# Channel attention and a gated convolution: eleven more rows of squares are summed on GpSimd instead of VectorE

## The chip, the cores and the metric

The kernel runs on one core of a Trainium2 chip. The metric is device time in microseconds (us) from one launch to its end. A time is the median of several runs; the profile and the trace come from one further execution of the same kernel, which has its own time.

## The reference

q, k and v have 4 batches of N = 6336 rows and C = 256 channels, in float32. The attention is over channels, so its matrix is 256x256 for a batch, and it can only be known when all 6336 rows of q and k of that batch have been read.

```
qn = q / (norm(q over rows) + 1e-6)          # one norm for each channel
kn = k / (norm(k over rows) + 1e-6)
s  = kn^T @ qn / tau                         # 256 x 256
a  = exp(s - max(s)); a /= sum(a) + 1e-9     # softmax over a row
x  = v @ a
gate = sigmoid(causal convolution of x over 5 rows, one filter for each channel)
out  = (gate * (x @ w_val)) @ w_out
```

## The kernel before

**Scores.** The rows of q and k of a batch are read as 49 rows for each of 128 partitions, and a rest of 64 rows. They are cut into 17 groups: group 0 has one row of 128 partitions and the rest, groups 1 to 16 have three rows each. `score_group` (lines 167 to 234) handles one group. For the later batches (1 to 3) it splits each row in a high and a low part: ScalarE casts the group to `hi` (L193), GpSimd subtracts for the low part (L194). TensorE multiplies three products for each half of the channels and each row into `s_ps` (L227), which stays in one bank for the whole batch. The norms need the sum of the squares of all rows: ScalarE squares the group into `sq` (L210, for the first row of a sum directly into the sum, L206), and the rows of `sq` are added up (L215) in one of two sums. The first `nv` rows of a group go to VectorE and its sum `acc_ps` in PSUM, the others to GpSimd and its sum `acc` (`side`) in SBUF. Line 175 sets `nv`: 1 in groups 1 to 4 of batch 1, and 2 in all other groups of the later batches.

**Softmax.** `softmax(b)` (L237 to L301) follows the last group of a batch: the two sums are added (L241), a matmul with ones sums them over the partitions (L246, L248), ScalarE takes the root (L253), VectorE the reciprocals (L258, L259), `nk` (L261), the scaled scores `s` (L264) and their minimum `m` (L266). ScalarE takes the exponential of the two halves of `s` (L269), VectorE adds 1e-9 to the sums `z` (L271) and inverts them (`rz`, L273), ScalarE scales to `a` (L276). TensorE transposes `a` in two pairs of matmuls with `ident` (L286), ScalarE copies the result to `at` (L290), and TensorE multiplies it with `w_val` (L295).

**Convolution.** The rows of v go through in 13 chunks of up to 508 rows for each batch, 52 steps in all. A step holds `conv` of the next chunk (L353: products `x_ps`, L346, in two buffers; ScalarE's first tap, L360; four more taps on VectorE, L362), the sigmoid of this chunk on ScalarE (L368), `value` (products `val_ps`, L346; VectorE multiplies the gate, L375), `split_g` (ScalarE casts `g_hi`, L388, GpSimd subtracts for `g_lo`, L389), the transposes of a coming chunk (`t_ps`, L336; `v_hi` on ScalarE, L337, `v_lo` on VectorE, L338), and `finish` of the chunk before (products `o_ps`, L405; ScalarE copies `o_sb`, L415).

**Order.** The main loop (L529 to L564) spreads the groups of the later batches over the first 36 steps, and each call of `tick()` issues one stage of a softmax at a raised priority. The order on each engine is not the order of the code: a scheduler places each instruction by its own model of their times, once, when the kernel is built. A change of one instruction's engine can so move others on all engines. On the chip each engine runs its instructions strictly in that order. Where ScalarE goes from one of Sqrt, Exp and Sigmoid to another, a table load (ACT_TABLE_LOAD, put down to the line of the function) stands ahead of the function.

Of the kernel before, what the change touches and what calls it, by code (L numbers as in the profile page):

```python
# [18 lines left out]
GROUP = 3  # L19
LEAD = 5  # L20
PREFETCH = 4
AHEAD = 2
VLEAD = 2
SIDE = 11
HALO = 4
# [4 lines left out]
def kernel(  # L30
# [25 lines left out]
    a_p = ctx.enter_context(tc.tile_pool(name="a_p", bufs=2))  # L56
    v_p = ctx.enter_context(tc.tile_pool(name="v_p", bufs=VLEAD + 1))
    w_p = ctx.enter_context(tc.tile_pool(name="w_p", bufs=2))
# [108 lines left out]
    def score_group(b, g):  # L167


        n = groups[g][1]  # L170
        raw = raws.pop((b, g))
        if b == 0:
            nw, nv = (GROUP, 2) if g < SIDE else (2, 3)
        else:
            nw, nv = (GROUP, 1 if g else 2) if b == 1 and g < LEAD else (0, 2)
        parts = [(P, 0, n)]
        if g == 0 and REST:
            parts.append((REST, n, 1))
        if g == 0:
            state[b] = dict(  # L180
                s=ps_s.tile([P, NH, C], F32, name="s_ps"),
                acc=ps_s.tile([P, 2, C], F32, name="acc_ps"),
                side=acc_p.tile([P, 2, C], F32, name="acc"),
                begun=set(),
            )
        st = state[b]
        split = [(np_, max(j0, nw), j0 + nj) for np_, j0, nj in parts if j0 + nj > nw]
        hi = split_p.tile([P, GROUP, 2, 2, C], F32R, name="hi") if split else None
        sq = split_p.tile([P, GROUP, 2, C], F32, name="sq", bufs=2)
        cast = None  # L190
        for np_, ja, jb in split:
            r, js = slice(0, np_), slice(ja, jb)
            cast = nc.scalar.copy(hi[r, js, :, 0, :], raw[r, js, :, :])  # L193
            nc.gpsimd.tensor_tensor(hi[r, js, :, 1, :], raw[r, js, :, :], hi[r, js, :, 0, :].bitcast(F32), ALU.subtract)  # L194
        rows = [(np_, j) for np_, j0, nj in parts for j in range(j0, j0 + nj)]
        where = {}
        with tc.issue_after(cast.ins) if cast else nullcontext():
            squares = [(np_, j0, j0 + nj) for np_, j0, nj in parts]
            for key in ("acc", "side"):
                if key not in st["begun"]:  # L200

                    full = [j for np_, j in rows if np_ == P and (j < nv) == (key == "acc")]
                    if full:
                        st["begun"].add(key)
                        where[full[0]] = key
                        nc.scalar.activation(st[key], raw[:, full[0]], AF.Square)  # L206
                        squares = [(np_, x, y) for np_, ja, jb in squares
                                   for x, y in ((ja, min(jb, full[0])), (max(ja, full[0] + 1), jb)) if x < y]
            for np_, ja, jb in squares:
                nc.scalar.activation(sq[0:np_, ja:jb], raw[0:np_, ja:jb], AF.Square)  # L210
        for np_, j in rows:
            if j in where:
                continue
            eng, key = (nc.vector, "acc") if j < nv else (nc.gpsimd, "side")
            eng.tensor_tensor(st[key][0:np_], st[key][0:np_], sq[0:np_, j], ALU.add)  # L215

        def mms(np_, j):
            r = slice(0, np_)
            stop = g == NG - 1 and np_ == parts[-1][0] and j == parts[-1][1] + parts[-1][2] - 1
            for h in range(NH):  # L220
                hs = slice(h * P, (h + 1) * P)
                if j < nw:
                    ops = [(raw[r, j, 1, hs], raw[r, j, 0, :])]
                else:
                    ops = [(hi[r, j, 1, x, hs], hi[r, j, 0, y, :]) for x, y in ((0, 0), (0, 1), (1, 0))]
                for n_, (lhs, rhs) in enumerate(ops):
                    nc.tensor.matmul(st["s"][:, h, :], lhs, rhs, start=False,  # L227
                                     stop=stop and h == NH - 1 and n_ == len(ops) - 1)

        def clear():  # L230

            nc.tensor.matmul(st["s"].rearrange("p h c -> p (h c)"), zeros[:, 0:P], zeros, start=True, stop=False)

        return ([clear] if g == 0 else []) + [lambda np_=np_, j=j: mms(np_, j) for np_, j0, nj in parts for j in range(j0, j0 + nj)]
# [76 lines left out]
    def load_v(b, i):  # L311

        t0, w = chunks[i]
        t = raw_p.tile([P, NT, C], F32, name="v_raw", bufs=3)
        j0 = 0
        if i == 0:
            nc.gpsimd.memset(t[0:HALO, 0, :], 0.0)
            nc.sync.dma_start(out=t[HALO:P, 0, :], in_=v[b, 0:P - HALO])
            j0 = 1
        full, rest = divmod(HALO + w, P)  # L320
        lo = t0 - HALO
        nc.sync.dma_start(out=t[:, j0:full, :], in_=v[b, lo + j0 * P:lo + full * P].rearrange("(j p) c -> p j c", p=P))
        if rest:
            nc.sync.dma_start(out=t[0:rest, full, :], in_=v[b, lo + full * P:t0 + w])
        vraw[b, i] = t
# [107 lines left out]
    @contextmanager  # L433
    def behind(*engines):
        with ExitStack() as st:
            for e in engines:
                st.enter_context(tc.issue_after(marks[e].ins))
            yield
# [7 lines left out]
    def split_group():  # L446
        nonlocal issued
        if issued < len(all_groups):
            b, g = all_groups[issued]
            issued += 1  # L450
            load_upto(issued + PREFETCH)
            ready.append((b, g, score_group(b, g)))
# [20 lines left out]
    def step(n):  # L473
        return all_steps[n] if 0 <= n < len(all_steps) else None


    for n in range(NG):
# [4 lines left out]
        if n == NG - 4:  # L482
# [4 lines left out]
            with tc.issue_after(last_load[0].ins):  # L487
                for nv in range(1, VLEAD + 1):
                    load_v(*step(nv))
# [33 lines left out]
    with behind("ACT"):  # L523
        for _ in range(AHEAD):
            split_group()
# [3 lines left out]
    for n in range(len(all_steps)):  # L529
        now, after, prev, new = step(n), step(n + 1), step(n - 1), step(n + VLEAD)  # L530
        if step(n + VLEAD + 1):
            load_v(*step(n + VLEAD + 1))
        due = NG + LEAD + -(-(total - NG - LEAD) * (n + 1) // (last + 1))
# [64 lines left out]
```

## Time and profile before

| what | value |
|---|---|
| median of 3 runs | 657.21 us (656.62 to 658.57) |
| profiled execution | 658.16 us, of which its span 656.4 us |
| granted TensorE clock, mean | 0.997 |
| TensorE busy (matmuls) | 637.9 us |
| VectorE busy | 524.5 us |
| ScalarE busy | 466.4 us |
| GpSimd busy | 360.6 us |

PE is TensorE, DVE VectorE, ACT ScalarE, POOL GpSimd. An engine's idle time counts for the whole only where the chain of work that ends last goes through it. Times in the trace are from the start of the span.

### The profile page before, as it was taken

Reading aid. Unit: us, or ns where it says so; the run is one execution under the profiler, and the core shown is the slowest. Engines: PE = TensorE matmul, PEld = TensorE weight load, DVE = VectorE, ACT = ScalarE, POOL = GpSimd, SP = SyncE. Lnnn points to the kernel's source line nnn. Section 1 sums busy time; section 2 is a strip of 40 time slices with the busy share of each in tenths; the row PEclk is TensorE's granted clock in tenths of the full one; section 3 lists DMA queues with packets and bytes.
Section 4 is the critical chain, followed back from the end, with each engine's and each line's share of the span. In section 5 each row is a group of like instructions: output and inputs, shape, how many; then the busy total and the mean of one; then the engine's idle time right before and its main releaser. Section 6 shows DMA issues by size and latency. Waiting matters only on the chain.

```text
span 656.4 us, 10675 instructions
## 1 busy us (share of the span) xinstructions
PE 637.9 (97%) x4008; PEld 571.5 (87%) x4008; DVE 524.5 (80%) x832; ACT 466.4 (71%) x607; POOL 360.6 (55%) x173
## 2 busy tenths in 40 slices
PE   7989999999999999999998999999999899999996
PEld 5878799999989999999997898998998698888886
DVE  3897689788689698877888588778788879888894
ACT  5465997876889778768689678777767755655554
POOL 2441898864846768749655397766753122212220
PEclk9999999999999999999999999999999999999999
DMA  8999875555555665455554365542323343343213
GB/s 269 334 326 343 253 228 186 163 151 170 165 151 151 188 199 171 142 164 172 169 166 143 108 208 179 179 137 78 91 75 96 96 126 103 113 129 105 65 51 97
DMA packets 107874, 105.75 MB, mean 161 GB/s; under 512 B 5744, under 2 KB 107312, under 8 KB 107824
## 3 DMA queue, kind: packets, MB, share of 16 engines
q1 hardware_dynamic: 81520, 79.24, 39.0%
q10 hardware_dynamic: 26304, 25.84, 14.0%
q8 instruction: 31, 0.51, 0.3%
q14 instruction: 19, 0.16, 0.1%
HBM read 79.11 MB, written 25.95 MB: 160 GB/s over the span
## 4 chain that ended last, share of the span: by engine, by line
PE 79%; ACT 6%; SPq 5%; DVE 4%; DMA 4%; issue 1%; POOL 1%; ACTq 0%; POOLq 0%
PE o_ps L405 20%; PE x_ps L346 19%; PE val_ps L346 19%; PE s_ps L227 13%; PE t_ps L336 6%; SPq L75 4%; DMA raw<-in_k_dram 2%; DVE gate L362 2%; ACT sq L210 1%; DMA v_raw<-in_v_dram 1%; PE o_ps L295 1%; ACT s L269 1%; DVE v_lo L338 1%; ACT gate L368 1%; POOL hi L194 1%
## 5 line engine op out<-in xcount | busy, mean ns | idle before, releaser
L362 DVE SCALAR_TENSOR_TENSOR gate<-x_ps,wa,gate 128x508 f32<-128x508 f32 (+1 forms) x416 | 276.6, 716 | 13.2 <-ACT gate L360 11.4
L194 POOL TENSOR_TENSOR hi<-raw,hi 128x1536 fp32r<-128x1536 f32 (+2 forms) x54 | 167.9, 3113 | 88.5 <-ACT hi L193 83.4
L389 POOL TENSOR_TENSOR g_lo<-gate,g_hi 128x1016 fp32r<-128x1016 f32 (+1 forms) x50 | 116.4, 2327 | 151.8 <-ACT g_hi L388 151.8
L215 DVE TENSOR_TENSOR acc_ps<-acc_ps,sq 128x512 f32<-128x512 f32 (+1 forms) x134 | 93.4, 697 | 73.6 <-ACT sq L210 70.3
L346 PE MATMUL x_ps<-v_hi,w 128*128 128x512 f32 (+1 forms) x416 | 140.3, 395 | 3.8 <-DVE gate L362 3.8
L346 PE MATMUL val_ps<-v_hi,w 128*128 128x508 f32 (+1 forms) x416 | 134.5, 383 | 0.1
L227 PE MATMUL s_ps<-hi 128*128 128x256 f32 (+1 forms) x852 | 125.9, 288 | 3.0 <-POOL hi L194 1.9
L227 PEld LDWEIGHTS s_ps<-hi 128*128 128x128 f32 (+1 forms) x852 | 112.8, 190 | 9.7 <-POOL hi L194 2.8
L415 ACT COPY o_sb<-o_ps 128x512 f32<-128x512 f32 x99 | 58.3, 588 | 82.8 <-PE o_ps L405 81.0
L405 PE MATMUL o_ps<-wo_hi,g_hi 128*128 128x256 f32 x400 | 113.1, 283 | 3.1 <-ACT at L290 1.6
L405 PE MATMUL o_ps<-wo_lo,g_hi 128*128 128x256 f32 x400 | 112.1, 281 | 0.0
L405 PE MATMUL o_ps<-wo_hi,g_lo 128*128 128x256 f32 x400 | 111.6, 280 | 0.0
L210 ACT ACTIVATE sq<-raw 128x1536 f32<-128x1536 f32 (+3 forms) x69 | 96.0, 1392 | 16.0 <-DMA raw<-in_k_dram 8.0
L215 POOL TENSOR_TENSOR acc<-acc,sq 128x512 f32<-128x512 f32 x58 | 76.6, 1321 | 39.0 <-ACT sq L210 38.6
L346 PEld LDWEIGHTS x_ps<-v_hi,w 128*128 128x128 f32 x416 | 77.9, 190 | 19.5 <-DVE gate L362 2.8
L346 PEld LDWEIGHTS val_ps<-v_hi,w 128*128 128x128 f32 x416 | 77.1, 188 | 13.4 <-DVE w L300 0.3
L360 ACT ACTIVATE gate<-x_ps,wa 128x508 f32<-128x508 f32 (+1 forms) x104 | 68.3, 668 | 24.5 <-PE x_ps L346 23.0
L346 PE MATMUL x_ps<-v_lo,w 128*128 128x512 f32 (+1 forms) x208 | 80.0, 385 | 0.0
L375 DVE TENSOR_TENSOR gate<-val_ps,gate 128x508 f32<-128x508 f32 (+1 forms) x104 | 64.2, 656 | 18.8 <-ACT gate L368 15.2
L346 PE MATMUL val_ps<-v_lo,w 128*128 128x508 f32 (+1 forms) x208 | 79.2, 381 | 0.0
L405 PEld LDWEIGHTS o_ps<-wo_hi,g_hi 128*128 128x128 f32 x400 | 75.2, 188 | 4.4 <-ACT at L290 2.0
L405 PEld LDWEIGHTS o_ps<-wo_lo,g_hi 128*128 128x128 f32 x400 | 75.3, 188 | 0.6
(84 smaller groups left out, 785.0 us busy)
## 6 DMA issues: line engine op xcount, KB each, us to landing
raw<-in_q_dram SPq DMA_DIRECT2D x64, 384.0 KB
raw<-in_k_dram SPq DMA_DIRECT2D x64, 384.0 KB
v_raw<-in_v_dram SPq DMA_DIRECT2D x44, 512.0 KB
out_dram<-o_sb ACTq DMA_DIRECT2D x48, 384.0 KB
out_dram<-o_sb ACTq DMA_DIRECT2D x48, 124.0 KB
v_raw<-in_v_dram SPq DMA_DIRECT2D x4, 384.0 KB
raw<-in_q_dram SPq DMA_DIRECT2D x4, 128.0 KB
raw<-in_k_dram SPq DMA_DIRECT2D x4, 128.0 KB
```

What stands on the lines that cost most here:

```text
L194: nc.gpsimd.tensor_tensor(hi[r, js, :, 1, :], raw[r, js, :, :], hi[r, js, :, 0, :].bitcast(F32), ALU.subtract)
L210: nc.scalar.activation(sq[0:np_, ja:jb], raw[0:np_, ja:jb], AF.Square)
L215: eng.tensor_tensor(st[key][0:np_], st[key][0:np_], sq[0:np_, j], ALU.add)
L227: nc.tensor.matmul(st["s"][:, h, :], lhs, rhs, start=False, stop=stop and h == NH - 1 and n_ == len(ops) - 1)
L336: nc.tensor.transpose(tp[:, j * P:j * P + np_], src[0:np_, j, h * P:(h + 1) * P], ident[0:np_, 0:np_])
L346: nc.tensor.matmul(ps, wt[:, which, ws, ch, hs], vs[:, ch, lo:hi_], start=n_ == 0, stop=n_ == 3 * NH - 1)
L360: nc.scalar.activation(gate[:, h, 0:w], x_ps[:, 0:w], AF.Copy, scale=cw[:, h, 0:1])
L362: nc.vector.scalar_tensor_tensor(gate[:, h, 0:w], x_ps[:, tap:tap + w], cw[:, h, tap:tap + 1], gate[:, h, 0:w], ALU.mult, ALU.add)
L375: nc.vector.tensor_tensor(gate[:, h, 0:w], val_ps[:, 0:w], gate[:, h, 0:w], ALU.mult)
L389: nc.gpsimd.tensor_tensor(gl[:, :, 0:w], gate[:, :, 0:w], gh[:, :, 0:w].bitcast(F32), ALU.subtract)
L405: nc.tensor.matmul(o_ps[:, u * C:(u + 1) * C], gs[:, h, off:off + P], ws[:, h, :], start=n_ == 0, stop=n_ == 3 * NH - 1)
L415: marks["ACT"] = nc.scalar.copy(o_sb[:, j:j + len(pair), :], o_ps[:, 0:len(pair) * C].rearrange("p (j c) -> p j c", c=C))
```

## The change

`nv` becomes 1 in groups 1 to 5 of each of the later batches. Batch 1 had it in groups 1 to 4 already, so eleven groups change: group 5 of batch 1, and groups 1 to 5 of batches 2 and 3. In each of them one row of squares (128x512) is added on GpSimd instead of VectorE. In group 1 of batches 2 and 3 GpSimd's sum now starts one row earlier, with a square of its own straight into the sum. The new constant takes a line, so that all lines behind it have a number higher by one in the changed kernel.

```diff
 AHEAD = 2
+BESIDE = 6
 VLEAD = 2
...
         else:
-            nw, nv = (GROUP, 1 if g else 2) if b == 1 and g < LEAD else (0, 2)
+            nw, nv = (GROUP, 1 if g else 2) if b == 1 and g < LEAD else (0, 1 if 0 < g < BESIDE else 2)
```

The scheduler also orders other instructions anew. Three places follow, each before and after.

**ScalarE in the softmax of batch 1, before.** `s` is the score matrix in its exponential, `gate` the sigmoid and the convolution's first tap, `a` the softmax's result.

```order
L269 ACT_TABLE_LOAD
L269 ACTIVATE s_1706,o_ps_1719<-s_1706,m_1773 128x256 x2
L368 ACT_TABLE_LOAD
L368 ACTIVATE gate_1724<-gate_1724 128x1016
L360 ACTIVATE gate_1862<-x_ps_1863,wa_109 128x508
L276 ACTIVATE a_1858<-s_1706,rz_1856 128x256 x2
L360 ACTIVATE gate_1862<-x_ps_1875,wa_109 128x508
L388 CAST g_hi_1911<-gate_1724 128x1016
L279 CAST w_1887<-a_1858 128x512
```

The same place with the change:

```order
L270 ACT_TABLE_LOAD
L270 ACTIVATE s_1706,o_ps_1720<-s_1706,m_1774 128x256
L369 ACT_TABLE_LOAD
L369 ACTIVATE gate_1725<-gate_1725 128x1016
L270 ACT_TABLE_LOAD
L270 ACTIVATE s_1706,o_ps_1720<-s_1706,m_1774 128x256
L361 ACTIVATE gate_1863<-x_ps_1864,wa_109 128x508
L361 ACTIVATE gate_1863<-x_ps_1876,wa_109 128x508
L389 CAST g_hi_1912<-gate_1725 128x1016
L277 ACTIVATE a_1859<-s_1706,rz_1857 128x256 x2
L280 CAST w_1888<-a_1859 128x512
```

The sigmoid and its table now stand between the two halves of the exponential. The second half needs a third table load, and both taps and the cast `g_hi` stand ahead of `a`, where one tap did. A further load of the sigmoid's table comes later. On TensorE the first pair of transposes of `a` stays behind the next chunk's convolution and 17 score matmuls; the second pair moves behind the first twelve matmuls of `finish`.

**ScalarE in the softmax of batch 2, before.** `gate` with `x_ps` is the first tap of the next chunk, in two halves.

```order
L360 ACTIVATE gate_3602<-x_ps_3603,wa_109 128x508
L360 ACTIVATE gate_3602<-x_ps_3615,wa_109 128x508
L388 CAST g_hi_3654<-gate_3444 128x1016
L269 ACT_TABLE_LOAD
L269 ACTIVATE s_3509,o_ps_3538<-s_3509,m_3634 128x256 x2
```

The same place with the change:

```order
L361 ACTIVATE gate_3604<-x_ps_3605,wa_109 128x508
L338 CAST v_hi_3660<-t_ps_3662 128x512
L389 CAST g_hi_3656<-gate_3445 128x1016
L270 ACT_TABLE_LOAD
L270 ACTIVATE s_3510,o_ps_3540<-s_3510,m_3636 128x256
L361 ACTIVATE gate_3604<-x_ps_3617,wa_109 128x508
L270 ACTIVATE s_3510,o_ps_3540<-s_3510,m_3636 128x256
```

The tap of the second half moves from ahead of `g_hi` to between the two halves of the exponential. No table load is added here. On TensorE four score matmuls move from ahead of the matmuls of the `finish` before this place to behind them.

**VectorE in the softmax of batch 2, before.** `m` is the minimum of the scaled scores, the two `x_ps` numbers the two halves of a chunk's taps, `o_ps` (128x2) first `z`, then `rz`.

```order
L266 TENSOR_REDUCE m_3634<-s_3509 128x2
L362 SCALAR_TENSOR_TENSOR gate_3602<-x_ps_3603,wa_109,gate_3602 128x508
L362 SCALAR_TENSOR_TENSOR gate_3602<-x_ps_3615,wa_109,gate_3602 128x508
L362 SCALAR_TENSOR_TENSOR gate_3602<-x_ps_3603,wa_109,gate_3602 128x508
L271 TENSOR_SCALAR o_ps_3538<-o_ps_3538 128x2
L362 SCALAR_TENSOR_TENSOR gate_3602<-x_ps_3615,wa_109,gate_3602 128x508
L338 TENSOR_TENSOR v_lo_3659<-t_ps_3667,v_hi_3658 128x512
L362 SCALAR_TENSOR_TENSOR gate_3602<-x_ps_3603,wa_109,gate_3602 128x508
L273 RECIPROCAL rz_3675<-o_ps_3538 128x2
L362 SCALAR_TENSOR_TENSOR gate_3602<-x_ps_3615,wa_109,gate_3602 128x508
L362 SCALAR_TENSOR_TENSOR gate_3602<-x_ps_3603,wa_109,gate_3602 128x508
```

The same place with the change:

```order
L267 TENSOR_REDUCE m_3636<-s_3510 128x2
L363 SCALAR_TENSOR_TENSOR gate_3604<-x_ps_3605,wa_109,gate_3604 128x508
L339 TENSOR_TENSOR v_lo_3661<-t_ps_3662,v_hi_3660 128x512
L363 SCALAR_TENSOR_TENSOR gate_3604<-x_ps_3605,wa_109,gate_3604 128x508
L363 SCALAR_TENSOR_TENSOR gate_3604<-x_ps_3617,wa_109,gate_3604 128x508
L363 SCALAR_TENSOR_TENSOR gate_3604<-x_ps_3605,wa_109,gate_3604 128x508
L272 TENSOR_SCALAR o_ps_3540<-o_ps_3540 128x2
L363 SCALAR_TENSOR_TENSOR gate_3604<-x_ps_3617,wa_109,gate_3604 128x508
L339 TENSOR_TENSOR v_lo_3661<-t_ps_3669,v_hi_3660 128x512
L363 SCALAR_TENSOR_TENSOR gate_3604<-x_ps_3605,wa_109,gate_3604 128x508
```

Between the minimum and `z` stand four taps and a `v_lo`, where three taps stood (that `v_lo` stood ahead of the minimum). Further ahead, not shown, one of two sums (L215) is gone. Behind `z` two taps and one `v_lo` lead to the last tap of the first half, where four taps, `v_lo` and `rz` did.

## Rows read from the trace of the kernel before

**Rows 1.** The page: busy time by engine (share, instructions), and the chain that ended last.

```profile
PE 637.9 (97%) x4008; PEld 571.5 (87%) x4008; DVE 524.5 (80%) x832; ACT 466.4 (71%) x607; POOL 360.6 (55%) x173
...
PE 79%; ACT 6%; SPq 5%; DVE 4%; DMA 4%; issue 1%; POOL 1%; ACTq 0%; POOLq 0%
```

**Rows 2.** Busy time by stretch: stretch, length, then each engine, clock, DMA share, GB/s.

```profile
164.00:202.00 38.00, 36.89 (x247) 33.41 (x246) 30.18 (x48) 33.18 (x48) 22.95 (x11) 1.00 0.53 153
202.00:335.00 133.00, 133.00 (x885) 121.45 (x884) 106.84 (x170) 100.71 (x125) 95.74 (x42) 1.00 0.55 168
335.00:364.00 29.00, 26.66 (x165) 23.75 (x164) 23.79 (x40) 26.13 (x37) 16.65 (x8) 0.94 0.53 157
364.00:505.00 141.00, 141.00 (x937) 128.82 (x936) 112.75 (x179) 102.76 (x129) 89.61 (x39) 1.00 0.44 130
505.00:535.00 30.00, 27.83 (x181) 24.28 (x180) 24.13 (x47) 21.52 (x37) 7.88 (x4) 1.00 0.37 109
```

**Rows 3.** Costliest groups: count, busy us, mean ns of one, idle before and its releaser.

```profile
L215 DVE TENSOR_TENSOR acc_ps<-acc_ps,sq 128x512 f32<-128x512 f32 (+1 forms) x134 | 93.4, 697 | 73.6 <-ACT sq L210 70.3
...
L415 ACT COPY o_sb<-o_ps 128x512 f32<-128x512 f32 x99 | 58.3, 588 | 82.8 <-PE o_ps L405 81.0
...
L215 POOL TENSOR_TENSOR acc<-acc,sq 128x512 f32<-128x512 f32 x58 | 76.6, 1321 | 39.0 <-ACT sq L210 38.6
```

**Rows 4.** TensorE's timeline, softmax of batch 1: start, length, instruction, [idle before, releaser].

```profile
192.66 0.50 PE L346 MATMUL x_ps<-v_hi,w 128*128 128x512 f32 x1 [0.96 <-DVE gate L362]
...
195.50 2.19 PE L227 MATMUL s_ps<-hi 128*128 128x256 f32 x17
197.53 0.38 PE L286 MATMUL o_ps<-ident,a 128*128 128x128 f32 x2
...
200.57 0.39 PE L405 MATMUL o_ps<-wo_hi,g_hi 128*128 128x256 f32 x1 [0.15 <-ACT at L290]
```

**Rows 5.** ScalarE's timeline, softmax of batch 1.

```profile
191.32 1.28 ACT L269 ACT_TABLE_LOAD   x1
192.62 0.51 ACT L269 ACTIVATE s<-s,m 128x256 f32<-128x256 f32 x1
...
193.22 0.51 ACT L269 ACTIVATE s<-s,m 128x256 f32<-128x256 f32 x1
...
193.80 1.28 ACT L368 ACT_TABLE_LOAD   x1
195.10 1.05 ACT L368 ACTIVATE gate<-gate 128x1016 f32<-128x1016 f32 x1
196.06 0.67 ACT L360 ACTIVATE gate<-x_ps,wa 128x508 f32<-128x508 f32 x1
196.62 0.90 ACT L276 ACTIVATE a<-s,rz 128x256 f32<-128x256 f32 x2
...
197.99 1.03 ACT L388 CAST g_hi<-gate 128x1016 fp32r<-128x1016 f32 x1
```

**Rows 6.** TensorE's timeline, softmax of batch 3.

```profile
519.33 0.39 PE L405 MATMUL o_ps<-wo_hi,g_hi 128*128 128x256 f32 x1 [1.41 <-ACT at L290]
```

**Rows 7.** TensorE's timeline, softmax of batch 2.

```profile
358.62 0.77 PE L346 MATMUL x_ps<-v_hi,w 128*128 128x512 f32 x1 [2.34 <-DVE gate L362]
```

**Rows 8.** Busy time by stretch (columns as in rows 2), behind that wait.

```profile
358.60:362.00 3.40, 3.38 (x9) 2.73 (x10) 1.93 (x3) 3.37 (x5) 3.40 (x2) 0.50 0.33 79
```

**Rows 9.** ScalarE's timeline, softmax of batch 2: the exponential.

```profile
353.83 0.51 ACT L269 ACTIVATE s<-s,m 128x256 f32<-128x256 f32 x1
...
354.43 0.51 ACT L269 ACTIVATE s<-s,m 128x256 f32<-128x256 f32 x1
```

**Rows 10.** VectorE's timeline, softmax of batch 2.

```profile
347.39 0.70 DVE L215 TENSOR_TENSOR acc_ps<-acc_ps,sq 128x512 f32<-128x512 f32 x1 [1.25 <-ACT sq L210]
...
352.15 2.04 DVE L362 SCALAR_TENSOR_TENSOR gate<-x_ps,wa,gate 128x508 f32<-128x508 f32 x3
355.03 0.17 DVE L271 TENSOR_SCALAR o_ps<-o_ps 128x2 f32<-128x2 f32 x1 [0.84 <-ACT s L269]
```

## The prediction, made before the changed kernel was run

> **What bounds the kernel now.** I read the page's busy times and chain first: TensorE is busy for 97% of the span and holds 79% of the chain, VectorE has 80% and 4%, GpSimd 55% and 1% [rows 1]. So TensorE sets the time, and VectorE's load, which this change lightens, is not the limit on average. Next comes the busy time by stretch, which shows where TensorE is not full [rows 2]. From 202 to 335 us and from 364 to 505 us it is busy for 133.00 of 133.00 and 141.00 of 141.00 us at clock 1.00; these stretches hold most of the changed groups. It loses 1.11 us between 164 and 202 and 2.34 us, at a mean clock of 0.94, between 335 and 364, where the softmax of batch 1 and that of batch 2 lie, and 2.17 us between 505 and 535, where that of batch 3 lies, whose order the change leaves as it was. Only in the first two can another engine's order cost or give time. So the timelines of those places come last: for batch 1 TensorE waits 0.96 us ahead of the next chunk's convolution and 0.15 us in `finish` [rows 4]; for batch 2 it waits 2.34 us ahead of the convolution [rows 7].
>
> **The moved adds themselves.** VectorE loses 11 adds of 0.70 us, 7.7 us, and GpSimd gains 11 of 1.32 us, 14.5 us [rows 3]. The square that is cut in two in group 1 of batches 2 and 3 costs ScalarE at most one more instruction of 0.59 us each, by the nearest row of that width, the copy `o_sb` [rows 3]. All of it lies beside TensorE, which has no wait there; GpSimd is busy for 95.74 of 133 us [rows 2]. The cover that I count on is TensorE's own work; were it gone, the low parts `hi` of a group would come later by one add, 1.3 us. Bounds 0 and 1.3 us a group at worst, and I take 0, because TensorE is full in both stretches where ten of these groups lie. Nor can the 7.7 us be a gain there.
>
> **Batch 1, the new order of ScalarE.** This is the costly part, and it is no part of the edit, but of the order that follows from it. First TensorE's side. It reaches the first transposes of `a` at 197.53 [rows 4]. Its wait ahead of the convolution should go, since VectorE has one sum less in its way: from the 0.96 us of idle and the start of the pipeline I count 1.1 us, and one score matmul less, at 0.12 us (17 in the 2.03 us from 195.50 to 197.53). So it arrives at 196.3. Then ScalarE's side, by start to start in its timeline [rows 5]. Its table load begins at 191.32, when the squares end. Four score matmuls stand newly ahead of the `finish` that feeds the copies ahead of it, 0.5 us, so 191.8. Then in the new order: load 1.30, half an exponential 0.59 (192.62 to 193.80 is two), load 1.30, sigmoid 0.96, load 1.30, the other half 0.59, two taps of 0.56, `g_hi` 1.03, half of `a` 0.45. That is 8.6 us, so `a` is there at 200.4. In the old order it took from 191.32 to about 197.1. TensorE now waits 200.4 - 196.3 = 4.1 us, and begins the transposes 200.4 - 197.5 = 2.9 us later than before. The second pair of transposes now stands directly ahead of the second half of `finish`, which waits for the copy `at`, as in row 200.57. That wait was 0.15 us here and 1.41 us in batch 3 [rows 4, 6]; I take the middle, 0.8, as ScalarE is behind by then. Sum: **+3.7 us**, with bounds 0 (everything ready in time) and 4.3.
>
> **The clock behind that wait.** Behind the 2.34 us wait of batch 2 the granted clock was 0.50, the lower level of 1.2 GHz, for 3.40 us, so 1.7 us were lost [rows 8]. With the 1.41 us wait of batch 3 [rows 6] the stretch around it kept clock 1.00 [rows 2]. A wait of 4.1 us is beyond the first of them: **+1.7 us**, bounds 0 and 1.7.
>
> A rule of the Trainium skill speaks for more: "ScalarE: Activation LUTs", section "What ACT_TABLE_LOAD costs", puts each switch of tables at about 2.66 us, 1.28 us for the load and 1.38 for a drain. By it the extra load ahead of `a` would cost 1.4 us more than I count, and the whole would come out at +4.1 us instead of +2.7. The trace has 1.28 us for the load, and the exponential starts 0.02 us behind its end [rows 5], so the measurement decides for 1.30.
>
> **Batch 2, what is given back.** TensorE's wait of 2.34 us ends when VectorE has done the last tap of the first half [rows 7]. It is tempting to credit the sum that is gone, since VectorE waits 1.25 us for squares ahead of it [rows 10]. But behind that VectorE waits again, 0.84 us for the exponential, which stands at 353.83 and 354.43 on ScalarE [rows 9, 10]; so ScalarE sets `z`. There one tap less stands ahead of the table load (0.56 us, of which I count 0.4, as `g_hi` then waits for VectorE) and four score matmuls less ahead of `finish` (0.5 us): the first half starts at 352.9. Half an exponential and the tap that now stands behind it, 0.59 + 0.56, lead to 354.1, and the two taps of VectorE that need this one, 2 x 0.68 by row 352.15, to `z` at 355.5, 0.4 us later than before. From `z` to the convolution it took 358.62 - 355.03 = 3.59 us, with two taps and `rz` (1.44 us) that no longer stand there: 2.15. So the convolution starts at 357.6: **-1.0 us**, bounds 0 and -2.3. The wait that is left, 1.3 us, is below the 1.41 us that kept the full clock, so the 1.7 us of half clock should go too: **-1.7 us**, bounds 0 and -1.7.
>
> **The sum.** 3.7 + 1.7 - 1.0 - 1.7 = +2.7 us. The profiled execution took 658.16 us (span 656.4 and 1.8 around it), so it would become 660.9; it lies 0.95 us above the median of 657.21, and on the median's footing the forecast is **659.9 us**. Its own range, from no loss of clock in batch 1 (+1.0) to the clock lost in both (+4.4), is 658.2 to 661.6. A difference below 0.3%, 2.0 us, can't be told from none here: 655.2 to 659.2 counts as the same.
>
> **Rivals.**
> - *The second half of the exponential is hidden, and only batch 2's gain is left: faster.* It decides whether `a` is there when TensorE arrives at 196.3. Then the 1.1 us ahead of the convolution is won, and 2.7 us in batch 2: -3.8, 653.4 us. For it: VectorE is less busy and the wait there was its own. Against: ScalarE is an engine that runs in order, and it would have to begin the load 4.1 us earlier, but the copies ahead of it wait for TensorE's own `finish`. Chance 0.12.
> - *The change does nothing to the time.* TensorE is full, the adds are beside it, and what batch 1 loses batch 2 returns (half clock in neither, batch 1's wait some 1.5 us, because VectorE or a load on ScalarE comes sooner than I count). 0, 657.2 us. For it: 274 us without one wait [rows 2]. Against: the third table load is in the order and can't be skipped. Chance 0.16.
> - *Batch 1 loses in full and batch 2 gives nothing back.* If `z` in batch 2 comes over a microsecond later than I count, as it now stands behind a tap that stands behind the exponential, the wait stays above 2.3 us with its half clock: +5.4, 662.6 us. For it: my -1.0 is the difference of two sums of about ten terms. Chance 0.13.
> - *A drain behind each load,* as the page cited above has it: with each switch at the 1.30 us of [rows 5] plus 1.38, +4.1 us, 661.3. The row speaks against it. Chance 0.03.
>
> **How the numbers follow.** The forecast has a chance of 0.56, its neighbours those above. A tenth of all cases are forecasts that end below 659.2, as without the loss of clock in batch 1. So faster has 0.13 (the first rival, and a little of the second), the same 0.27 (the second rival and that tenth, less the little), slower 0.60. The range is 656.0 to 663.0 us: it leaves out the first rival and the outer end of the third, and takes in the rest.
>
> **What would show it.** In the trace of the changed kernel: 17 table loads where there were 15; TensorE without a wait ahead of the convolution near 191.5, but with one of about 4 us ahead of the transposes of `a` (L287) near 196, released by `a` (L277), and half the clock for some 3 us behind it; near 357 a wait of about 1.3 us at full clock; from 210 to 335 and from 370 to 505 us a full TensorE as before; VectorE's group L216 smaller by 11 and 7.7 us, GpSimd's larger by 11 and 14.5 us. I would be wrong if the transposes do not wait, if the wait of batch 2 stays above 2 us with its half clock, or if TensorE waits for `hi` of GpSimd (L195) in the groups that changed.

## The result and the profile after

The changed kernel took 660.46 us (median of 6 runs, 659.66 to 661.66); the kernel before, in 6 runs beside it, 657.72 us (656.62 to 658.57). The ratio is 1.0042, 95% interval 1.0028 to 1.0057: 2.7 us slower. The forecast was +2.7 us (659.9 us for a base of 657.21), in a range of 656.0 to 663.0.

The page of the changed kernel, busy time by engine and the chain, for [rows 1]:

```profile
PE 637.2 (97%) x4008; PEld 571.0 (87%) x4008; DVE 515.8 (78%) x821; ACT 469.4 (71%) x611; POOL 374.9 (57%) x184
...
PE 86%; ACT 5%; SPq 3%; DMA 2%; issue 1%; DVE 1%; POOL 1%; ACTq 0%; POOLq 0%
```

VectorE is 8.7 us lighter, GpSimd 14.3 us heavier, and VectorE has left the chain but for 1%. The relief that the edit asks for is there, and the time went up. Groups of the changed kernel, for [rows 3]:

```profile
L216 POOL TENSOR_TENSOR acc<-acc,sq 128x512 f32<-128x512 f32 x69 | 91.0, 1318 | 37.8 <-ACT sq L211 37.0
L216 DVE TENSOR_TENSOR acc_ps<-acc_ps,sq 128x512 f32<-128x512 f32 (+1 forms) x123 | 85.8, 697 | 81.0 <-ACT sq L211 78.2
...
L369 ACT ACT_TABLE_LOAD x8 | 10.3, 1283 | 1.0 <-ACT o_sb L416 0.9
L270 ACT ACT_TABLE_LOAD x4 | 5.1, 1283 | 0.9 <-ACT o_sb L416 0.9
```

Before, the two groups of table loads were:

```profile
L368 ACT ACT_TABLE_LOAD x7 | 9.0, 1283 | 1.0 <-ACT o_sb L415 0.9
L269 ACT ACT_TABLE_LOAD x3 | 3.8, 1283 | 0.9 <-ACT o_sb L415 0.9
```

Eleven adds went over, and one load of the sigmoid's table (L369) and one of the exponential's (L270) came in. Busy time by stretch, for [rows 2] and, in the last two lines, [rows 8]:

```profile
164.00:210.00 46.00, 41.49 (x258) 37.41 (x257) 32.88 (x53) 37.74 (x53) 26.31 (x14) 0.96 0.44 132
210.00:335.00 125.00, 125.00 (x844) 114.63 (x843) 99.59 (x159) 94.03 (x118) 94.12 (x43) 1.00 0.56 171
335.00:364.00 29.00, 27.58 (x179) 24.74 (x179) 22.19 (x38) 26.70 (x38) 20.16 (x11) 1.00 0.57 166
364.00:505.00 141.00, 140.99 (x937) 128.59 (x936) 110.56 (x174) 105.09 (x131) 95.82 (x44) 1.00 0.44 131
199.30:202.70 3.40, 3.40 (x16) 3.40 (x17) 3.40 (x6) 2.12 (x4) 1.96 (x1) 0.50 0.02 5
361.30:365.00 3.70, 3.63 (x17) 3.02 (x18) 2.09 (x4) 3.68 (x5) 3.33 (x1) 1.00 0.46 124
```

TensorE is as full as before in the two long stretches that hold most of the moved adds. It loses 4.5 us in batch 1's softmax, where it lost 1.1, and has half the clock there for 3.4 us. In batch 2's softmax it loses 1.4 us instead of 2.3 and keeps the clock. TensorE's timeline at these places, for [rows 4, 7]:

```profile
190.27 0.40 PE L347 MATMUL x_ps<-v_hi,w 128*128 128x512 f32 x1
...
199.28 0.69 PE L287 MATMUL o_ps<-ident,a 128*128 128x128 f32 x2 [4.05 <-ACT a L277]
...
204.29 0.39 PE L406 MATMUL o_ps<-wo_hi,g_hi 128*128 128x256 f32 x1 [0.46 <-ACT o_sb L416]
...
361.37 0.47 PE L347 MATMUL x_ps<-v_hi,w 128*128 128x512 f32 x1 [1.42 <-DVE rz L274]
```

The wait ahead of batch 1's convolution is gone, and a longer one stands ahead of the transposes of `a`. ScalarE's timeline shows why, for [rows 5]:

```profile
190.63 1.28 ACT L270 ACT_TABLE_LOAD   x1
191.93 0.51 ACT L270 ACTIVATE s<-s,m 128x256 f32<-128x256 f32 x1
...
192.52 1.28 ACT L369 ACT_TABLE_LOAD   x1
193.81 1.05 ACT L369 ACTIVATE gate<-gate 128x1016 f32<-128x1016 f32 x1
194.88 1.28 ACT L270 ACT_TABLE_LOAD   x1
196.18 0.51 ACT L270 ACTIVATE s<-s,m 128x256 f32<-128x256 f32 x1
...
196.64 1.25 ACT L361 ACTIVATE gate<-x_ps,wa 128x508 f32<-128x508 f32 x2
197.78 1.04 ACT L389 CAST g_hi<-gate 128x1016 fp32r<-128x1016 f32 x1
198.70 0.92 ACT L277 ACTIVATE a<-s,rz 128x256 f32<-128x256 f32 x2
```

From the first table load to `a` it now takes 8.07 us, where it took 5.30 (191.32 to 196.62).

One warning on reading the two profiles. Their spans, 656.4 and 657.9 us, differ by 1.5 us only, because the part ahead of the first convolution, which has the same instructions in both, took 1.25 us less in the execution that was profiled after. TensorE's first convolution and its last matmul, of before and of after:

```profile
69.95 0.47 PE L346 MATMUL x_ps<-v_hi,w 128*128 128x512 f32 x1
...
652.00 0.28 PE L405 MATMUL o_ps<-wo_hi,g_lo 128*128 128x256 f32 x1
```

```profile
68.70 0.48 PE L347 MATMUL x_ps<-v_hi,w 128*128 128x512 f32 x1
...
653.54 0.28 PE L406 MATMUL o_ps<-wo_hi,g_lo 128*128 128x256 f32 x1
```

Between these it is 582.05 us before and 584.84 us after, +2.8 us, as in the medians. The runs below are compared over the same stretch where single executions are compared.

### The profile page after: what moved, and what is told of

Its sections match the earlier page's. It is cut to its first block, busy times and chain, and to the rows that moved or that the text cites. A ratio compares the mean times of both kernels' runs of the same rounds, so it can differ in the third digit from the quotient of the medians.

```text
span 657.9 us, 10690 instructions
## 1 busy us (share of the span) xinstructions
PE 637.2 (97%) x4008; PEld 571.0 (87%) x4008; DVE 515.8 (78%) x821; ACT 469.4 (71%) x611; POOL 374.9 (57%) x184
## 4 chain that ended last, share of the span: by engine, by line
PE 86%; ACT 5%; SPq 3%; DMA 2%; issue 1%; DVE 1%; POOL 1%; ACTq 0%; POOLq 0%
PE o_ps L406 21%; PE x_ps L347 20%; PE val_ps L347 19%; PE s_ps L228 18%; PE t_ps L337 6%; SPq L76 2%; DMA raw<-in_k_dram 2%; PE o_ps L296 1%; ACT L270 1%; POOL hi L195 1%; ACT sq L211 1%; ACT L369 1%; ACT g_hi L389 0%; DVE gate L363 0%; ACT gate L361 0%
## 5 line engine op out<-in xcount | busy, mean ns | idle before, releaser
L363 DVE SCALAR_TENSOR_TENSOR gate<-x_ps,wa,gate 128x508 f32<-128x508 f32 (+1 forms) x416 | 277.7, 718 | 10.8 <-ACT gate L361 8.9
L216 DVE TENSOR_TENSOR acc_ps<-acc_ps,sq 128x512 f32<-128x512 f32 (+1 forms) x123 | 85.8, 697 | 81.0 <-ACT sq L211 78.2
L216 POOL TENSOR_TENSOR acc<-acc,sq 128x512 f32<-128x512 f32 x69 | 91.0, 1318 | 37.8 <-ACT sq L211 37.0
L211 ACT ACTIVATE sq<-raw 128x1536 f32<-128x1536 f32 (+2 forms) x71 | 96.3, 1359 | 14.6 <-DVE acc_ps L216 7.2
L361 ACT ACTIVATE gate<-x_ps,wa 128x508 f32<-128x508 f32 (+1 forms) x104 | 68.0, 667 | 20.0 <-PE x_ps L347 19.3
L338 ACT CAST v_hi<-t_ps 128x512 fp32r<-128x512 f32 (+1 forms) x104 | 55.9, 568 | 29.6 <-PE t_ps L337 29.6
```

The lines of the kernel that those rows point to most:

```text
L338: nc.scalar.copy(th[:, h, 0:w], tp[:, 0:w])
L361: nc.scalar.activation(gate[:, h, 0:w], x_ps[:, 0:w], AF.Copy, scale=cw[:, h, 0:1])
L363: nc.vector.scalar_tensor_tensor(gate[:, h, 0:w], x_ps[:, tap:tap + w], cw[:, h, tap:tap + 1], gate[:, h, 0:w], ALU.mult, ALU.add)
```

## The experiments

Two theories were set against each other. The order theory is that of the prediction: the edit's own work is hidden, and the order that the scheduler makes of it costs and gives time in the two softmaxes. The load theory: GpSimd's added work costs the time, by late low parts or by slowing VectorE. Differences are against the kernel before, run on the same chip in the same series.

**Batch 1's order without the edit.** In the kernel before, for batch 1 only:

```diff
         for h in range(NH):
-            marks["ACT"] = nc.scalar.activation(s[:, h, :], s[:, h, :], AF.Exp, scale=-1.0, bias=m[:, h:h + 1], accum_out=z[:, h:h + 1])
-        yield
+            if b == 1 and h:
+                yield
+                yield
+            with tc.issue_after(marks["sig"].ins) if b == 1 and h else nullcontext():
+                marks["ACT"] = nc.scalar.activation(s[:, h, :], s[:, h, :], AF.Exp, scale=-1.0, bias=m[:, h:h + 1], accum_out=z[:, h:h + 1])
+        if b != 1:
+            yield
...
-        nc.scalar.activation(gate[:, :, 0:w], gate[:, :, 0:w], AF.Sigmoid)
+        marks["sig"] = nc.scalar.activation(gate[:, :, 0:w], gate[:, :, 0:w], AF.Sigmoid)
```

> The kernel before, no row of squares moved; only in the softmax of batch 1 the second half of the exponential is issued behind the next sigmoid, so that ScalarE's order there is that of the change (17 table loads for 15). Order theory (ScalarE's order in batch 1's softmax costs the time): TensorE waits 3 to 4 us for `a`, half the clock for 3 to 4 us behind it, batch 2's wait of 2.3 us stays: +4.0 to +5.5 us against the kernel before. Load theory (the adds on GpSimd cost the time): no add is moved, so 0 within 1 us.

Measured: 660.74 against 658.01 us, ratio 1.0043 (1.0029 to 1.0057), +2.7 us. TensorE's timeline of this run:

```profile
194.31 0.50 PE L352 MATMUL x_ps<-v_hi,w 128*128 128x512 f32 x1 [0.95 <-DVE gate L368]
...
201.63 0.44 PE L292 MATMUL o_ps<-ident,a 128*128 128x128 f32 x2 [2.29 <-ACT a L281]
...
364.22 0.47 PE L352 MATMUL x_ps<-v_hi,w 128*128 128x512 f32 x1 [2.33 <-DVE gate L368]
```

No add was moved, and the kernel is 2.7 us slower. This refutes the load theory as the whole cause, but the size missed my range: VectorE is not relieved here, so the wait ahead of the convolution stays, TensorE comes 1 us later to the transposes, and its wait there is 2.3 us instead of the 3 to 4 that I wrote. From the first convolution to the last matmul it is 584.35 us, +2.3. That the median difference equals that of the change is chance, as batch 2's wait is not shortened here. Up to batch 2's convolution this execution is 3.9 us behind that of before (364.22 - 71.62 against 358.62 - 69.95); 1.6 us of it come back behind that place, where this execution kept the full clock and that of before did not [rows 8].

**The change with its order repaired.** In the changed kernel the sigmoid is issued behind the second half of the exponential:

```diff
-            marks["ACT"] = nc.scalar.activation(s[:, h, :], s[:, h, :], AF.Exp, scale=-1.0, bias=m[:, h:h + 1], accum_out=z[:, h:h + 1])
+            marks["ACT"] = marks["exp"] = nc.scalar.activation(s[:, h, :], s[:, h, :], AF.Exp, scale=-1.0, bias=m[:, h:h + 1], accum_out=z[:, h:h + 1])
...
-        nc.scalar.activation(gate[:, :, 0:w], gate[:, :, 0:w], AF.Sigmoid)
+        e = marks.pop("exp", None)
+        with tc.issue_after(e.ins) if e else nullcontext():
+            nc.scalar.activation(gate[:, :, 0:w], gate[:, :, 0:w], AF.Sigmoid)
```

> The change in full, but the sigmoid is held behind both halves of the exponential, so that no table load is added (15). Order theory: TensorE arrives 1.1 us earlier at the transposes of batch 1 and waits about 1.2 us there at full clock, so batch 1 is worth 0, and batch 2 gives 2.6 us: -2.0 to -3.5 us against the kernel before. Load theory: the same eleven adds are on GpSimd, so the +2.7 us of the change stay.

Measured: 657.03 against 658.01 us, ratio 0.9986 (0.9978 to 0.9995), -1.0 us. TensorE's timeline:

```profile
198.45 0.44 PE L287 MATMUL o_ps<-ident,a 128*128 128x128 f32 x2 [1.24 <-ACT a L277]
...
202.33 0.39 PE L408 MATMUL o_ps<-wo_hi,g_hi 128*128 128x256 f32 x1 [0.93 <-ACT at L291]
...
359.62 0.47 PE L347 MATMUL x_ps<-v_hi,w 128*128 128x512 f32 x1 [1.40 <-DVE rz L274]
```

With all eleven adds on GpSimd the kernel is 3.7 us faster than the change (the two ratios, 0.9986 and 1.0042, on 658 us). The wait for `a` is the 1.2 us that I expected; the gain falls short of -2.0 because of a second wait in `finish`, 0.93 us for 0.15, and because batch 2's part is smaller than 2.6 us, which the next run shows by itself.

**Batch 2's and batch 1's order apart.** The line that sets `nv`, with `b != 2 and 0 < g < BESIDE` in the one run and `b == 2 and 0 < g < BESIDE` in the other. The groups of a batch are worked on while the softmax of the batch before runs, so batch 2's groups set batch 1's order and batch 3's set batch 2's.

> Only group 5 of batch 1 and groups 1 to 5 of batch 3 move a row (six of eleven); batch 1's softmax then has the order of the kernel before, batch 2's that of the change. Order theory: batch 2's wait near 357 us shrinks from 2.3 to about 1.4 us and keeps the clock: -2.0 to -3.0 us. Load theory: six of eleven adds, +1.5 us.

Measured: 656.29 against 658.01 us, ratio 0.9977 (0.9965 to 0.9990), -1.7 us.

> Only groups 1 to 5 of batch 2 move a row (five of eleven); batch 1's softmax has the order of the change (17 table loads), batch 2's that of the kernel before. Order theory: the wait of 4 us and its half clock are there, and so is batch 2's wait of 2.3 us with its own: +4.0 to +6.0 us. Load theory: five of eleven adds, +1.2 us.

Measured: 662.40 against 658.01 us, ratio 1.0071 (1.0058 to 1.0084), +4.4 us. TensorE's timelines, first without batch 2's groups, then with these alone, and a stretch of the latter:

```profile
192.27 0.50 PE L347 MATMUL x_ps<-v_hi,w 128*128 128x512 f32 x1 [0.96 <-DVE gate L363]
...
357.32 0.47 PE L347 MATMUL x_ps<-v_hi,w 128*128 128x512 f32 x1 [1.42 <-DVE rz L274]
```

```profile
200.32 0.69 PE L287 MATMUL o_ps<-ident,a 128*128 128x128 f32 x2 [4.05 <-ACT a L277]
...
363.85 0.47 PE L347 MATMUL x_ps<-v_hi,w 128*128 128x512 f32 x1 [2.34 <-DVE gate L363]
```

```profile
198.50:205.20 6.70, 4.88 (x23) 4.88 (x24) 6.70 (x11) 3.95 (x7) 2.36 (x1) 0.50 0.12 38
```

Each softmax's waits are those of the change where its order is, and those of before where not, to 0.01 us. The two medians add up: +4.4 - 1.7 = +2.7, the change. They do not separate the two batches cleanly, because the clock behind these waits differs from the change's: half of it for 6.7 us in batch 1, and all of it behind batch 2's 2.34 us. Five adds cost 4.4 us and six gain 1.7, so the count of adds says nothing. Batch 2's part is smaller than the 2.0 to 3.0 that I wrote.

**GpSimd's load without the edit.** In `score_group` of the kernel before, with `spare` a zeroed tile that nothing reads:

```diff
+        if (b == 1 and g == 5) or (b > 1 and 0 < g < 6):
+            for _ in range(2):
+                nc.gpsimd.tensor_tensor(spare, spare, sq[:, 1], ALU.add)
```

> The kernel before, with two further adds of 128x512 on GpSimd into a spare tile in each of the eleven groups that the change touches (22 adds, twice what the change puts there, 29 us of GpSimd); VectorE keeps its own, and the softmaxes keep their order. Order theory: all of it lies beside TensorE, 0 within 0.7 us. Load theory (GpSimd's work comes late for the low parts, or slows VectorE): twice the change's +2.7, so +5 us, with waits of TensorE for GpSimd's low parts.

Measured: 657.93 against 657.47 us, ratio 1.0003 (0.9993 to 1.0012). The group of the added work:

```profile
L221 POOL TENSOR_TENSOR spare<-spare,sq 128x512 f32<-128x512 f32 x22 | 29.0, 1320 | 0.3
```

Twice the change's load on GpSimd, 29.0 us, costs 0.2 us by the ratio, with an interval of 0.5 below to 0.8 above. From 80 us on TensorE waits only once for a low part of GpSimd in this run, for 0.5 us, as in the kernel before:

```profile
PE s_ps L233 <- POOL hi L196: 0.5, 1, 0.5
```

The load theory falls.

**Two adds of the eleven.** `BESIDE = 2`.

> The change cut down to group 1 of batches 2 and 3 (two adds of eleven). ScalarE's order in batch 1's softmax is that of the change (17 table loads), in batch 2's both taps stand ahead of the exponential. Order theory: batch 1 costs what it cost with five groups of batch 2, +4.4 us, and batch 2 gives back 1.7 to 2.3: +2.0 to +3.5 us. Load theory: two of eleven adds, +0.5 us.

Measured: 661.68 against 657.47 us, ratio 1.0065 (1.0052 to 1.0078), +4.2 us, above my range. TensorE's timeline:

```profile
200.86 0.69 PE L287 MATMUL o_ps<-ident,a 128*128 128x128 f32 x2 [4.04 <-ACT a L277]
...
362.17 0.47 PE L347 MATMUL x_ps<-v_hi,w 128*128 128x512 f32 x1 [0.71 <-DVE rz L274]
```

Two adds are enough for batch 1's order and its 4 us wait, and batch 2's wait falls to 0.7, below the 1.4 that five moved adds of batch 3 leave there. From the first convolution to the last matmul this run takes 584.74 us, +2.7, inside my range. A part of the median's further 1.5 us may lie in the base: the profiled execution of before lost the clock in batch 2, and 14 of the 20 runs of before in this series report a mean clock of 0.999 or 1.000, so that less could be given back in them. I have not resolved it further.

**The rest of batch 2's wait.** On the run without batch 2's groups, for batch 2 only, the exponential behind the first taps on ScalarE (L361) and `z` behind the last of VectorE's taps:

```diff
-            marks["ACT"] = nc.scalar.activation(s[:, h, :], s[:, h, :], AF.Exp, scale=-1.0, bias=m[:, h:h + 1], accum_out=z[:, h:h + 1])
+            with tc.issue_after(marks["g1"].ins) if b in (2,) else nullcontext():
+                marks["ACT"] = nc.scalar.activation(s[:, h, :], s[:, h, :], AF.Exp, scale=-1.0, bias=m[:, h:h + 1], accum_out=z[:, h:h + 1])
...
-        nc.vector.tensor_scalar(z, z, 1e-9, None, ALU.add)
+        with tc.issue_after(marks["tap"].ins) if b in (2,) else nullcontext():
+            nc.vector.tensor_scalar(z, z, 1e-9, None, ALU.add)
```

`marks["g1"]` and `marks["tap"]` are the last instructions that L361 and L363 have issued.

> As the run without batch 2's groups, and in batch 2's softmax the exponential behind both first taps of the chunk, and VectorE's `z` behind the last of its taps, so that the convolution's buffers wait for no exponential. Order theory: the wait of 1.4 us near 357 us falls to 0.5 us or less, no other appears: 0.9 to 1.5 us less than without batch 2's groups, so -2.5 to -3.3 us against the kernel before. If VectorE's load and not its order were what TensorE waits for, nothing changes: -1.7 us as there.

Measured: 659.21 against 657.47 us, ratio 1.0024 (1.0011 to 1.0037), +1.7 us: a miss. TensorE's timeline, a stretch behind it, and ScalarE's timeline:

```profile
356.82 0.47 PE L349 MATMUL x_ps<-v_hi,w 128*128 128x512 f32 x1 [0.52 <-DVE gate L365]
...
362.71 0.44 PE L289 MATMUL o_ps<-ident,a 128*128 128x128 f32 x2 [2.69 <-ACT a L279]
```

```profile
364.00:367.40 3.40, 3.40 (x11) 2.54 (x10) 3.40 (x6) 0.13 (x1) 0.09 (x1) 0.50 0.41 143
```

```profile
359.34 1.28 ACT L371 ACT_TABLE_LOAD   x1
360.63 1.05 ACT L371 ACTIVATE gate<-gate 128x1016 f32<-128x1016 f32 x1
361.59 0.67 ACT L363 ACTIVATE gate<-x_ps,wa 128x508 f32<-128x508 f32 x1
362.16 0.89 ACT L279 ACTIVATE a<-s,rz 128x256 f32<-128x256 f32 x2
```

The wait ahead of the convolution fell to 0.5 us as expected. But with a later `z` the scheduler put `a` behind the sigmoid, its table and a tap, and the wait came back ahead of the transposes, longer and with half the clock. It is the change's own mechanism in another batch.

**The same with `z` left in its place.** Only the exponential is held behind the first taps.

> As the run without batch 2's groups; in batch 2's softmax only the exponential is held behind both first taps of the chunk, `z` and `a` stay where they were. Order theory: the wait ahead of the convolution near 357 us falls from 1.4 to about 0.6 us, as in the run with group 1 alone, and no wait for `a` appears; 0.8 us less than without batch 2's groups, so -2.0 to -2.8 us against the kernel before. If the wait only moves behind the convolution, as it did when `z` was held back, the time stays at that of the kernel before or above.

Measured: 654.96 against 657.98 us, ratio 0.9960 (0.9947 to 0.9972), -3.0 us. TensorE's timeline:

```profile
357.29 0.47 PE L348 MATMUL x_ps<-v_hi,w 128*128 128x512 f32 x1 [0.72 <-DVE rz L275]
```

The wait fell by 0.7 us and none took its place; the gain is a little beyond the 2.0 to 2.8 that I wrote. This beats both kernels: six adds moved, and one order set by hand.

**The full change with both orders repaired.** The two edits of `exp`, on the changed kernel.

> The change in full (all eleven adds on GpSimd) with both halves of the exponential ahead of the sigmoid, and in batch 2 behind both first taps. Order theory: batch 1 as in the run with the exponential together (+1.1 us of waits of the kernel before), batch 2 with a wait of 0.6 us: -1.3 to -2.5 us against the kernel before, 4 us or more below the change as it stands. Load theory: +2.7 us.

Measured: 656.62 against 657.98 us, ratio 0.9983 (0.9973 to 0.9992), -1.4 us, at the small end of what I wrote. Batch 1 keeps its waits of 1.25 us for `a` and 0.93 us in `finish`; batch 2's is 0.71 us. The kernel is 3.9 us faster than the change by the two ratios, with the same eleven adds on GpSimd.

## Why the prediction was right

- **The moved adds cost nothing:** right. TensorE stays full in the long stretches, and 22 spare adds on GpSimd change the time by 0.2 us. From 80 us on TensorE never waits for GpSimd's low parts in the profile of the change. Counting VectorE's 7.7 us as a gain would have been the trap.
- **Batch 1's waits:** right in place, releaser and size. The wait ahead of the convolution went, and the one ahead of the transposes is 4.05 us, where 4.1 was worked out from rows of before. The run that splits the exponential and moves no add, and the one that moves all adds and doesn't split it, show that this order is the cause. The transposes begin 130.58 us behind the first convolution (199.28 - 68.70), 3.0 us later than before (197.53 - 69.95), for a forecast of 2.9. The second wait, in `finish`, is 0.46 us and not 0.8, and a copy `o_sb` ends it, not `at`; the sum also added the 0.8 in full, though 0.15 of it stood there before [rows 4].
- **Batch 1's clock:** the profiled run shows 3.4 us at half clock, as taken. The whole batch 1 term was put at +5.4 us. From the first convolution to the one that ends batch 2's wait it is 288.67 us before (358.62 - 69.95) and 292.67 with the change (361.37 - 68.70), with the same matmuls in between. That is +4.0, and batch 2's wait at its end is 0.9 us shorter, so batch 1 cost +4.9. The later transposes and the wait in `finish` make 3.3 of it; the 1.6 that are left fit with the 1.7 taken for the clock. The run with batch 2's groups alone has +5.5 up to that place (363.85 - 69.71), with its longer half clock.
- **The drain behind a table load:** the exponential starts at 196.18, 0.02 us behind the end of the load that began at 194.88. The case of the Trainium skill's "ScalarE: Activation LUTs" ("What ACT_TABLE_LOAD costs") with 2.66 us for a switch does not hold here; the cost was 1.30.
- **Batch 2's wait:** 1.42 us for a forecast of 1.3. ScalarE sets it, as argued: VectorE waits 1.12 us for the tap L361 that stands behind the first half of the exponential, as its timeline of the changed kernel shows. From `z` to the convolution it is 2.20 us (359.17 to 361.37), for 2.15. The profile names `rz` as what ended TensorE's wait; it stands directly behind the tap of the first half that the prediction names, which ends 0.14 us ahead of the convolution.

```profile
357.85 1.40 DVE L363 SCALAR_TENSOR_TENSOR gate<-x_ps,wa,gate 128x508 f32<-128x508 f32 x2 [1.12 <-ACT gate L361]
359.17 0.16 DVE L272 TENSOR_SCALAR o_ps<-o_ps 128x2 f32<-128x2 f32 x1
```

- **Batch 2's clock, "so the 1.7 us of half clock should go too":** this term was mis-sized, and the reason given for it, the shorter wait, is not shown. From the convolution that ends batch 2's wait to the last matmul it is 293.38 us before (652.00 - 358.62) and 292.17 with the change (653.54 - 361.37): 1.2 us came back, not 1.7. Every profiled execution with a wait of 1.42 us or less ahead of that convolution kept the clock there, but a shorter wait is not needed: the run with batch 2's groups alone waits 2.34 us there as the kernel before does, keeps the clock, and takes 292.25 us from there to its last matmul:

```profile
656.10 0.28 PE L406 MATMUL o_ps<-wo_hi,g_lo 128*128 128x256 f32 x1
```

The prediction also took one profiled execution of before for all of them. Of 56 runs of before in three series 32 report a mean granted clock of 0.997 (median 658.2 us) and the others 0.999 or 1.000 (657.2 us). The mean does not say where the clock was lost (below), but if the first are those that lost it in batch 2, an estimate is that 1.0 x 32 / 56 = 0.6 us is lost there in the mean. With the 0.9 us of the wait that is 1.5 us; measured, without batch 2's groups, 1.7.

The sum was right although both of its parts were too large, by about half a microsecond each and on opposite sides: +5.4 and -2.7 were put down, +4.9 and -2.1 came out in the two profiled executions, and +4.4 and -1.7 in the medians of the two runs that take the batches apart. That these errors cancel was luck. The chances are added up wrongly by 0.02: those listed give 0.25 for the same and 0.62 for slower. The first rival, with `a` in time, fell with its condition; the third, with nothing given back in batch 2, is refuted by the run without batch 2's groups. The condition of the second, that the parts cancel, was nearest, but batch 1 costs more than twice what batch 2 returns.

## What to carry to other kernels

Where a scheduler orders the instructions, the cost of an edit is not in the edit: compare the order on every engine, and look for a table load, a copy or a cast that now stands ahead of what the bound engine waits for. A load taken off an engine that the bound engine does not wait for gives nothing, and two adds can cost as much as eleven. When a change of 0.4% comes from order, hold the one pair that matters in place and keep the rest; and when an order is set by hand, look at the next wait behind it, as holding back `z` moved the wait instead of removing it.

## What the runs showed of the hardware that was not expected

- The same wait is not always followed by the lower clock. A wait of 2.34 us ahead of batch 2's convolution was followed by a granted clock of 0.50 and a first matmul of 0.77 us in the profiled execution of before [rows 7, 8], and by a first matmul of 0.47 us at full clock in the run with batch 2's groups alone (363.85 above); the run that splits the exponential has 2.33 us there and the full clock as well (364.22 above).
- The lower clock can last longer behind equal waits: 3.4 us behind the 4.05 us wait of the change, 6.7 us (to 205.20) around and behind the same 4.05 us in the run with batch 2's groups alone. Four of that run's five executions report a mean clock of 0.994, the change's six 0.995 to 0.997.
- The mean granted clock of an execution also counts the time behind TensorE's last matmul, so a lower mean alone does not show that TensorE lost anything. The profiled execution of the full change with both orders repaired reports 0.997, as that of before does, but has the full clock from 70 us to 650.40 and half of it only behind the last matmul, where TensorE does nothing:

```profile
650.80:654.50 3.70, 0.00 (x0) 0.00 (x0) 0.42 (x1) 0.37 (x1) 0.00 (x0) 0.50 0.32 98
```

- The start of the program varies by as much as this change costs: the first convolution's matmul starts at 68.70 us in the profile of after, at 69.95 in that of before and at 71.62 in that of the run that splits the exponential, and the instructions up to there are the same in all three.
